# Two more blocks of V kept across the layer change, with the feed-forward weights laid around them

## The chip, the cores and the metric

One Trainium2 chip, one of its cores. The time is that of the device, in microseconds (us), from one execution of the whole program; lower is better.

## The reference

Two layers, run twice with the same weights and the same caches: attention of one new token per sequence against cached keys and values, then a gated feed-forward. Four sequences (B = 4), width 512, 32 query heads in 8 groups, 8192 cached positions, head size 128.

```python
def _A_ref(x, k_cache, v_cache, wq, wo):
    q = (x @ wq).reshape(B, Sq, Hq, Dh).transpose(0, 2, 1, 3)
    k = jnp.repeat(k_cache, rep, axis=1)
    v = jnp.repeat(v_cache, rep, axis=1)
    scores = jnp.einsum("bhqd,bhkd->bhqk", q, k) * (Dh ** -0.5)
    p = _softmax(scores, axis=-1)
    o = jnp.einsum("bhqk,bhkd->bhqd", p, v)
    return o.transpose(0, 2, 1, 3).reshape(B, Sq, Hq * Dh) @ wo
def _B_ref(x, w_gate, w_up, w_down):
    return (_silu(x @ w_gate) * (x @ w_up)) @ w_down
x = x + _A_ref(_layernorm(x), A_k_cache, A_v_cache, A_wq, A_wo)
x = x + _B_ref(_layernorm(x), B_w_gate, B_w_up, B_w_down)
# and both lines once more
```

K and V are 67.1 MB each in bf16 and each layer needs all of both; the weights are small beside them (w_gate, w_up and w_down are 512 x 1792 or its reverse).

## The kernel before, in words

**Units.** A unit u (0 to 15) is one sequence and two of the 8 key groups. K(u) and V(u) are 4096 KB each: 128 partitions by 8 blocks of 4 KB, so one block of a transfer is 512 KB. Layer 0 takes the units in the order 0 to 15, layer 1 in the order 15, 14, 13, 12, 0, 1 ... 11 (`order`).

**Room.** `kvf` holds four slots (0 to 3) of 8 blocks for K and V, a fifth slot (`QS`) that holds wq first and serves as a fifth slot in layer 1, and `wres` for part of the up weights. The program tracks each block of each slot under a name (`s1.6` is block 6 of slot 1).

**The queue.** All transfers are written out in one list, `cmds`, made by `placed`: item, slot, first and last block. SyncE issues them in that order. `pump` goes on with the list whenever `freed` gives blocks back, and an issue waits on the chip for the last readers of its room, so one that waits holds up all behind it.

**A unit's work.** VectorE (DVE) turns keys in place (`turn`, two blocks at a time as a rule), TensorE (PE) makes the scores block by block (`scores`), DVE takes the maximum (`max_p`, `max_t`), ScalarE (ACT) the exponential (`exps`), DVE turns that into `pT` (`turn_p`), and PE multiplies it with V in four parts (`values`). For the last unit of a layer the turned exponential lies in `late_pT`, at the end of the slot of the weights, instead of `pT`. `keys` and `values` put blocks of PE's work into a list that `drain` empties some microseconds late (`LAG`, and `AHEAD` for the second unit of layer 1), so that DVE runs ahead; the steps behind a unit's scores lie in `line` and are dealt out between blocks by `advance`. Each engine works in the order in which it was given instructions.

**The layer change.** What layer 0 used last is kept for layer 1 (`keep`): K(15) in slot 0, V(14) in slot 2, V(15) in slot 3; and of K(13) blocks 6 and 7 are held in the matmul memory and turned back later (`hold`, `half_kept`). Slot 1, whose last tenant is V(13), takes the feed-forward weights as soon as V(13) is used: gate (7168 elements of a partition), the rest of up, then w_down in three pieces (`WDS`; the last, `W+`, when the last unit is done with `late_pT`). The feed-forward (`ffn`) makes gate, then up, each as 14 column blocks of 4 matmuls, then the down product in 56 matmuls; it gives slot 1 back piece by piece, for K(14). `qproj` then frees the two halves of `QS` for K(13), K(15)'s scores free slot 0 for K(12), K(14)'s free slot 1 for V(13). Layer 1 ends with its own weights in slot 3.

Below, K(14) and the like always mean the loads for layer 1 unless layer 0 is named.

Of the kernel before, what the change touches and what calls it, by code (L numbers as in the profile page):

```python
# [9 lines left out]
FP32 = mybir.dt.float32  # L10
# [93 lines left out]
def bass_interleave_layers__gqa_block_cached__swiglu_ffn__decode_kernel(  # L104
# [18 lines left out]
    P = 128  # L123
# [21 lines left out]
    with ExitStack() as es:  # L145
# [14 lines left out]
        WDS = (((0, 8, 4), (8, 12, 4), (12, 14, 2)), ((0, 8, 2), (8, 12, 2), (12, 14, 2)))  # L160
        NW = len(WDS[0])

# [3 lines left out]
        assert O_WD + FO * D <= SL  # L166
        wres = kvf[:, (NSLOT + 1) * SL:]
# [19 lines left out]
        def wd_at(s, fo, k):  # L187
            return columns(s * SL + O_WD + fo * D + pick2(k).start)

        pT_w = TB * NH * QB  # L190
        assert all((w[-1][1] - w[-1][0]) * D >= pT_w for w in WDS)

        def late_pT(s):
            return kvf[:, (s + 1) * SL - pT_w:(s + 1) * SL]
# [20 lines left out]
        pT = sb("pT", [P, TB, NH, QB], BF16)  # L215

# [138 lines left out]
        cmds += [(("W", 0), W_SLOT[0], 0, NB), (("W+", 0), W_SLOT[0], NB, NB + 1)]  # L355
# [9 lines left out]
        cmds += [(("W", 1), W_SLOT[1], 0, NB), (("W+", 1), W_SLOT[1], NB, NB + 1)]  # L365

# [4 lines left out]
        def load_weight(name, i=0, s=0):  # L371
            if name == "wq":
                n = 2 * HqDh
                T.dma("sp", kv[:, QS, i * n:(i + 1) * n],
                      A_wq[i * 2 * P:(i + 1) * 2 * P, :].rearrange("(p e) f -> p (e f)", e=2), sem_w["wq"][i],
                      writes=[f"wq{i}"])
            elif name == "wo":
                src = A_wo[i * H2 * Dh:(i + 1) * H2 * Dh, :]
                T.dma("sp", wo_sb[:, i * H2:(i + 1) * H2, :].rearrange("p (c j) n -> p c (j n)", j=NA),
                      src.rearrange("(c p j) n -> p c (j n)", p=P, j=NA), sem_w["wo"][i], writes=[f"wo{i}"])  # L380
            else:
                w0 = kvf[:, s * SL:(s + 1) * SL]
                if name == "W+":
                    load_wd(w0, i, NW - 1, ["late"])
                    return
                T._wait("pool", T._need((), [f"s{s}.{NB - 1}"]))
                T.op("pool", lambda e: e.memset(late_pT(s).bitcast(FP32), 0.0), writes=["late"])
                T.dma("sp", w0[:, 0:KT * F].rearrange("p (c x) -> p c x", c=2),
                      B_w_gate.rearrange("(c p e) f -> p c (e f)", c=2, e=2), sem_w["wg"][0],
                      writes=[f"s{s}.{q}" for q in range(NB)] + ["wg"])  # L390
# [6 lines left out]
                for j in range(NW - 1):  # L397
                    load_wd(w0, i, j)

        def load_wd(w0, L, j, also=()):  # L400
            a, b, e_ = WDS[L][j]
            T.dma("sp", w0[:, O_WD + a * D:O_WD + b * D].rearrange("p (m x) -> p m x", x=e_ * D),
                  B_w_down[a * P:b * P, :].rearrange("(m p e) n -> p m (e n)", p=P, e=e_), sem_w["wd"][j],
                  writes=[f"wd{j}"] + list(also))

        def pump(most=len(cmds)):
            while issued[0] < most:
# [3 lines left out]
                else:  # L411
                    need = {(s, q) for q in range(a, b)}
# [3 lines left out]
                    if it[0] in ("W", "W+"):  # L416
                        load_weight(it[0], it[1], s)
                    else:
                        slot_of[it] = s
                        load(it, a, b, sem_s[s] if b - a == NB else part_sem())  # L420
# [4 lines left out]
        def load(it, a, b, sm):  # L425
            kind, L, u = it
            s = slot_of[it]
            gp, bt = pair_gb(u)
# [4 lines left out]
            T.dma("sp", kv[:, s, a * BW:b * BW], src[:, a * BW:b * BW], sm,  # L433
                  writes=[f"s{s}.{q}" for q in range(a, b)] + over)
# [24 lines left out]
        def finished(it, a, b):  # L459
# [24 lines left out]
        def turn(L, u, q, n):  # L484
            s = slot_of[K(L, u)]
            w = kv[:, s, q * BW:(q + n) * BW].bitcast(FP32)
            names = [f"s{s}.{i}" for i in range(q, q + n)]
# [17 lines left out]
        def scores(L, u, q):  # L505

            s = slot_of[K(L, u)]
            bk = SBK[turn_of[u]]
            w = kv[:, s, q * BW:(q + 1) * BW].rearrange("p (t c i e) -> p t c i e", t=TB, c=2, e=2)
            for c in range(4):  # L510
# [3 lines left out]
                     reads=[f"s{s}.{q}", "zq"], writes=[f"pb{bk}"], sig=(c == 3))  # L514
# [51 lines left out]
        def pT_of(L, u):  # L566
            if u == order[L][-1]:
                return late_pT(W_SLOT[L]).rearrange("p (t n x) -> p t n x", n=NH, x=QB), "late"
# [29 lines left out]
        def keys(L, u, before, lag):  # L598
# [14 lines left out]
            for q in range(NB):  # L613
                if (L, u, q) not in turned:
                    two = 0 < order[L].index(u) < NP - 1 and q % 2 == 0 and (L, u, q + 1) not in turned
# [11 lines left out]
        def values(L, u):  # L627
# [22 lines left out]
            def part(i):  # L650
# [18 lines left out]
                if i == 3:  # L669
                    more = later.pop(0)() if later else []  # L670
                    if p_name == "late":
                        freed(W_SLOT[L], NB, NB + 1)
                    done.add((L, u))
# [191 lines left out]
        def ffn(L):  # L865
# [6 lines left out]
            rooms = {"wg": room(s, 0, O_WU), "wu": room(s, O_WU, O_WD)}  # L872
            for j, (a, b, _) in enumerate(WDS[L]):
                rooms[f"wd{j}"] = room(s, O_WD + a * D, O_WD + b * D)
            names = {"wg": ["wg"], "wu": ["wu0", "wu1", "wu2"]}
            for at, wname, bk in ((wg_at, "wg", gb), (wu_at, "wu", ub)):
                for fo in range(FO):
                    if bk == gb and fo == FO // 2:
                        deviation(zero_sb, "zero")
                    f = base(L, fo)  # L880
                    for kt in range(KT):
# [3 lines left out]
                                                      start=(kt == 0), stop=(kt == KT - 1)),  # L885
                             reads=rooms[wname] + names[wname] + ["xn"], writes=[f"pb{bk}"],
                             sig=(fo == FO - 1 and kt == KT - 1))
                freed(s, *((0, 3) if wname == "wg" else (3, 4)))
# [20 lines left out]
            for j, (a, b, _) in enumerate(WDS[0]):  # L909
                k = OBK[0] if j else SBK[1]  # L910
                for nt in range(KT):
                    for fo in range(a, b):
# [3 lines left out]
                                                      start=(j < 2 and nt == 0 and fo == a),  # L916
                                                      stop=(j in (0, NW - 1) and nt == KT - 1 and fo == b - 1)),
# [86 lines left out]
```

## Time and profile before

| | before |
|---|---|
| time, median of 3 runs | 647.07 us (646.84 to 647.4) |
| profiled execution | 647.03 us, span 645.1 us from the first to the last instruction |
| mean granted clock of TensorE | 0.827 |
| transfers on the list in the layer change, W to V(13) | 19 |

The page of the profile gives the busy time of each engine, the span in 40 slices, the DMA queues, the chain of work that ended last, the costliest groups of instructions and the DMA issues. Times in the timeline and the chain are in us from the span's start. "L488" is line 488 of the kernel before: L488 turns keys, L512 is the scores' matmul, L518 the maximum, L644 the product with V, L841 qproj, L882 gate and up, L913 the down product of layer 0, L903 that of layer 1, L453 the turning back of held keys, L93 the helper that issues every transfer. A row of DMA issues ends with the time from issue to landing; a transfer has landed when the last of the 16 DMA engines is done with its part.

### The profile page before, as it was taken

The page shows a single profiled execution, that of the slowest core. Times are in us where ns is not written, and L with a number is a line of the kernel's source. Part 1 is how long each engine was busy: PE and PEld are TensorE (multiplying, and loading weights), DVE is VectorE, ACT ScalarE, POOL GpSimd, SP SyncE. Part 2 cuts the span into 40 slices and gives each one's busy share as a digit, 9 for nine tenths or more (in the row PEclk, how much of TensorE's full clock was granted, in tenths as well). Part 3 has the DMA queues.
Part 4 walks back from the last instruction along what each step waited for, and adds up shares of the span by engine and source line. Part 5 has one row for each costly group of instructions (what it writes and reads, how often), then busy time and mean ns, then how long its engine had stood idle before and what let it go on. Part 6 is the DMA issues. An engine that isn't in the chain of part 4 may idle for free.

```text
span 645.1 us, 7412 instructions
## 1 busy us (share of the span) xinstructions
PE 419.5 (65%) x3126; PEld 182.6 (28%) x3128; DVE 422.0 (65%) x591; ACT 41.2 (6%) x117; POOL 11.1 (2%) x43
## 2 busy tenths in 40 slices
PE   0683475456765746767867877777555676557877
PEld 0431122122222312222226433233122222222325
DVE  5275467456776656776962778878655677665964
ACT  0000000000000000000010010000000000000110
POOL 0000000000000000000000000000000000000000
PEclk9995887688876889767975899997778887679787
DMA  9999999999999999999999999999999999999997
GB/s 368 442 425 418 440 434 425 426 433 438 425 425 440 433 424 432 435 431 424 433 412 404 424 446 424 425 438 432 425 428 443 424 427 439 432 427 426 441 410 276
DMA packets 14704, 273.36 MB, mean 424 GB/s; under 512 B 1480, under 2 KB 1488, under 8 KB 5328
## 3 DMA queue, kind: packets, MB, share of 16 engines
q1 hardware_dynamic: 14672, 272.91, 99.1%
q8 instruction: 24, 0.39, 0.2%
q14 instruction: 8, 0.07, 0.0%
HBM read 272.90 MB, written 0.00 MB: 423 GB/s over the span
## 4 chain that ended last, share of the span: by engine, by line
DMA 62%; DVE 20%; PE 12%; issue 3%; another core or an unknown queue 1%; SPq 0%; ACTq 0%; ACT 0%; DVEq 0%
DMA kvf<-in_A_k_cache_dram 50%; DVE kvf L488 16%; DMA kvf<-in_A_v_cache_dram 11%; PE ps L512 7%; PE ps L644 2%; DMA kvf<-in_B_w_down_dram 2%; DVE pb L694 2%; PE ps L841 1%; PE ps L882 0%; DVE pb L690 0%; DVE kvf L453 0%; DVE scr L704 0%; SPq L93 0%; PE ps L523 0%
## 5 line engine op out<-in xcount | busy, mean ns | idle before, releaser
L512 PE MATMUL ps<-kvf,zq 128*128 128x512 bf16 x1024 | 297.0, 437 | 182.0 <-DVE kvf L488 178.2
L488 DVE STREAM_TRANSPOSE kvf<-kvf 128x2048 f32<-128x2048 f32 (+1 forms) x131 | 280.0, 2162 | 127.8 <-DMA kvf<-in_A_k_cache_dram 127.6
L512 PEld LDWEIGHTS ps<-kvf,zq 128*128 128x128 bf16 x1024 | 100.7, 109 | 339.7 <-DVE kvf L488 218.7
L644 PE MATMUL ps<-kvf,pT 128*32 128x512 bf16 x960 | 65.8, 396 | 1.3 <-DVE pT L576 1.3
L559 ACT ACTIVATE pb<-ps,tiny 128x512 bf16<-128x512 f32 x32 | 22.0, 688 | 529.7 <-DVE tiny L557 510.0
L576 DVE STREAM_TRANSPOSE pT<-pb 64x512 bf16<-64x512 bf16 x60 | 41.2, 687 | 3.6 <-ACT pb L559 2.6
L694 DVE SCALAR_TENSOR_TENSOR pb<-ps,tiny,pb 128x128 f32<-128x128 f32 x104 | 36.5, 351 | 4.5 <-PE ps L644 0.8
L518 DVE TENSOR_REDUCE tiny<-ps 128x1 f32<-128x512 f32 x32 | 22.0, 687 | 21.3 <-PE ps L512 21.3
L644 PEld LDWEIGHTS ps<-kvf,pT 128*32 128x32 bf16 x960 | 20.8, 98 | 31.0 <-issue 15.3
L699 PEld LDWEIGHTS ps<-sel,pb 128*128 128x128 f32 x64 | 17.3, 278 | 16.6 <-DVE pb L694 8.0
L502 POOL TENSOR_TENSOR zq<-scr,tiny 128x64 bf16<-128x64 bf16 x30 | 9.0, 299 | 563.3 <-PE ps L512 563.3
L526 DVE TENSOR_REDUCE mrm<-ps 1x8 f32<-1x128 f32 x32 | 8.8, 275 | 13.8 <-PE ps L523 13.8
L549 PEld LDWEIGHTS ps<-mrm,tiny 128*128 128x128 f32 x60 | 13.7, 234 | 9.6 <-issue 3.3
L699 PE MATMUL ps<-sel,pb 128*128 128x8 f32 x64 | 12.5, 269 | 5.5 <-DVE pb L694 5.5
L841 PE MATMUL ps<-xn,kvf 128*128 128x4 bf16 x256 | 7.4, 166 | 11.3 <-DMA kvf<-in_A_wq_dram 11.0
L549 PE MATMUL ps<-mrm,tiny 128*128 128x16 f32 x60 | 10.4, 251 | 3.1 <-ACT mrm L561 3.1
L690 DVE TENSOR_SCALAR pb<-ps,tiny 128x128 f32<-128x128 f32 x32 | 10.1, 316 | 2.6 <-PE ps L644 2.6
L760 PE MATMUL ps<-wo_sb,scr 128*4 128x512 bf16 x48 | 11.0, 379 | 0.4 <-DVE scr L729 0.4
L841 PEld LDWEIGHTS ps<-xn,kvf 128*128 128x128 bf16 x256 | 7.3, 105 | 11.6 <-DMA kvf<-in_A_wq_dram 11.2
L523 PE MATMUL ps<-identf,tiny 128*1 128x128 f32 x32 | 8.6, 270 | 1.9 <-DVE tiny L518 1.9
L561 ACT ACTIVATE mrm<-head,tiny 128x8 f32<-128x8 f32 x32 | 9.6, 300 | 1.0
L882 PE MATMUL ps<-xn,kvf 128*128 128x4 bf16 x224 | 7.3, 169 | 1.6 <-DMA kvf<-in_B_w_up_dram 1.2
(83 smaller groups left out, 113.1 us busy)
## 6 DMA issues: line engine op xcount, KB each, us to landing
kvf<-in_A_k_cache_dram SPq DMA_DIRECT2D x27, 4096.0 KB, 31.0
kvf<-in_A_v_cache_dram SPq DMA_DIRECT2D x27, 4096.0 KB, 35.3
kvf<-in_A_v_cache_dram SPq DMA_DIRECT2D x4, 2048.0 KB, 18.4
kvf<-in_A_k_cache_dram SPq DMA_DIRECT2D x7, 1024.0 KB, 9.9
kvf<-in_A_k_cache_dram SPq DMA_DIRECT2D x3, 2048.0 KB, 11.0
kvf<-in_A_wq_dram SPq DMA_DIRECT2D x2, 2048.0 KB, 18.1
wo_sb<-in_A_wo_dram SPq DMA_DIRECT2D x4, 1024.0 KB, 41.3
kvf<-in_B_w_gate_dram SPq DMA_DIRECT2D x2, 1792.0 KB, 23.7
```

The lines of the kernel that those rows point to most:

```text
L488: T.op("dve", lambda e: e.transpose(w, w), reads=names, writes=names)
L512: T.op("pe", lambda e: e.matmul(bank(bk)[:, 0:SW], lhsT=zq[:, z0:z0 + P], rhs=w[:, :, c // 2, :, c % 2], start=(q == 0 and c == 0), stop=( ...
L518: T.op("dve", lambda e: e.tensor_reduce(mx[:], bank(bk)[:, 0:SW], AX.X, ALU.max), reads=[f"pb{bk}"], writes=["mx"])
L549: T.op("pe", lambda e: e.matmul(at, lhsT=ones, rhs=mrm[:, i * H2:(i + 2) * H2], start=True, stop=True), reads=[f"m8{i}", "rsm", "onesf"], ...
L559: T.op("act", lambda e: e.activation(pb[:], bank(bk)[:, 0:SW], ACTF.Exp, bias=nm, accum_out=rs), reads=[f"pb{bk}", "nm"], writes=PB + ["rs"])
L576: T.op("dve", lambda e: e.transpose(dst, pb[hp]), reads=["pb", "row"], writes=[name])
L644: T.op("pe", lambda e: e.matmul(bank(k)[j * QB:(j + 1) * QB, q0 * Dh:q1 * Dh], lhsT=p_t[:, t, h, :], rhs=v[:, q0:q1, t, :], start=((last o ...
L690: T.op("dve", lambda e: e.tensor_scalar(into, o, own[:, q:q + 1], None, op0=ALU.mult), reads=[f"pb{k}", "own"], writes=["row"] if last els ...
L694: T.op("dve", lambda e: e.scalar_tensor_tensor(into, o, own[:, q:q + 1], into, op0=ALU.mult, op1=ALU.add), reads=[f"pb{k}", "own", iname], ...
L699: T.op("pe", lambda e: e.matmul(at, lhsT=into, rhs=sel[:], start=True, stop=True), reads=[iname, "sel"], writes=[name])
L760: T.op("pe", lambda e: e.matmul(bank(OUTB)[0:B, 0:D], lhsT=oT[:, h, :], rhs=wo_sb[:, h, :], start=(gp == groups[L][0] and r == 0), stop=(g ...
L841: T.op("pe", lambda e: e.matmul(at[:, h * B:(h + 1) * B], lhsT=wq_sb[:, kt, h * Dh:(h + 1) * Dh], rhs=xn[:, kt * B:(kt + 1) * B], start=(k ...
```

## The change

- **V(13).** Blocks 6 and 7 of V(13), which layer 0 left in slot 1, stay there (`parked`, `PARK` = 6). Layer 1 loads only blocks 0 to 5.
- **Weights of layer 0.** They now have 6 blocks of slot 1. w_down goes in five pieces: column blocks 8 to 11 and 12, 13 behind the up weights; 6 and 7 into `pT` (`Wp`, after V(14)'s product); 0 to 3 and 4, 5 (`W2`) over the first half of the gate weights, issued when that half has been used. The down product takes the pieces in this order, and GpSimd zeroes `pT` afterwards.
- **Keys of K(14).** Blocks 0 to 5 go to slot 1 in another order (2, then 3, then 4 and 5, then 0 and 1), blocks 6 and 7 to blocks 0 and 1 of slot 0 (`aside`, `home`, `lies`). They are turned singly, behind the scores of K(14)'s blocks 3 and 4 in the list of blocks. K(12)'s blocks 0 and 1, whose room that is, are loaded after V(13).
- **Gate and up.** Each is made in two halves of the contraction: the first half for all 14 column blocks, then the second half for all of them, each with names of its own to wait for. This holds for both layers.

```diff
-        WDS = (((0, 8, 4), (8, 12, 4), (12, 14, 2)), ((0, 8, 2), (8, 12, 2), (12, 14, 2)))
+        WDS = (((8, 12, 4), (12, 14, 2), (6, 8, 2), (0, 4, 4), (4, 6, 2)), ((0, 8, 2), (8, 12, 2), (12, 14, 2)))
...
+        PARK = NB - 2
+        ENDS = (PARK * BW, SL)
+        LATE = (1, 2)
+        FO_P, FO_S = WDS[0][2][:2]
+        QN = -(-FO_P * D // BW)
...
+        def wd_from(L, fo):
+            return O_WD + fo * D if L else fo * D if fo < FO_P else O_WD + (fo - FO_S) * D
...
-        cmds += [(("W", 0), W_SLOT[0], 0, NB), (("W+", 0), W_SLOT[0], NB, NB + 1)]
+        parked = {V(0, NP - 3): V(1, NP - 3)}
+        cmds += [(("W", 0), W_SLOT[0], 0, PARK), (("W+", 0), W_SLOT[0], NB, NB + 1),
+                 (("Wp", 0), W_SLOT[0], NB + 1, NB + 2)]
...
-        cmds += [(K(1, us[1]), s, a, b) for a, b in ((0, 3), (3, 4), (4, 6), (6, NB))]
+        cmds += [(("W2", 0), s, NB + 2, NB + 3)]
+        cmds += [(K(1, us[1]), s, a, b) for a, b in ((QN, 3), (3, 4), (4, PARK), (0, QN))]
         cmds += [(K(1, us[2]), QS, 0, NB // 2), (K(1, us[2]), QS, NB // 2, NB - 2)]
+        cmds += [(K(1, us[1]), 0, PARK, NB)]
         seq = loads(1, 3)
         ring = (0, 1, 3, QS, 2)
-        cmds += placed(seq, ring, {0: twos, 1: half, len(seq) - 1: ends})
+        n = NB - PARK
+        rest = placed(seq, ring, {0: lambda it, s: [(it, s, 0, n), (it, s, n, 4), (it, s, 4, 6), (it, s, 6, NB)],
+                                  1: lambda it, s: [(it, s, 0, QH), (it, s, QH, PARK)],
+                                  len(seq) - 1: ends})
+        cmds += rest[1:6] + rest[:1] + rest[6:]
...
+        aside = K(1, us[1])
+        def home(it, a, b):
+            if it == aside and a >= PARK:
+                return 0, a - PARK, b - PARK
+            return slot_of[it], a, b
...
+                if name == "W2":
+                    for j in range(3, len(WDS[i])):
+                        load_wd(w0, i, j, ["wg0"] if j == 3 else [])
+                    return
...
+            elif it in parked and b > PARK:
+                slot_of[parked[it]] = slot_of[it]
+                freed(slot_of[it], a, PARK)
             else:
-                freed(slot_of[it], a, b)
+                freed(*home(it, a, b))
...
-                if (L, u, q) not in turned:
+                if (L, u, q) not in turned and not (K(L, u) == aside and q >= PARK):
...
                 blocks.append((0.9, lambda q=q: block(q)))
+                if K(L, u) == aside and 3 <= q < 3 + NB - PARK:
+                    blocks.append((0.0, lambda q=q - 3 + PARK: turn(L, u, q, 1)))
...
-            for at, wname, bk in ((wg_at, "wg", gb), (wu_at, "wu", ub)):
+            for at, wname, bk, ks in ((wg_at, "wg0", gb, (0, KT // 2)), (wg_at, "wg1", gb, (KT // 2, KT)),
+                                      (wu_at, "wu0", ub, (0, KT // 2)), (wu_at, "wu1", ub, (KT // 2, KT))):
...
+                if wname == "wg0":
+                    deviation(zero_sb, "zero")
+                    if not L:
+                        freed(s, NB + 2, NB + 3)
+                elif wname[-1] == "1":
+                    freed(s, *((0 if L else QN, 3) if wname == "wg1" else (3, 4)))
...
             for j, (a, b, _) in enumerate(WDS[0]):
-                k = OBK[0] if j else SBK[1]
+                k = OBK[0] if j > 2 else SBK[1]
...
-                if not j:
-                    freed(s, 4, 6)
+                if j == 1:
+                    freed(s, 4, PARK)
+                if j == 2:
                     add_to_x(bank(k)[:, 0:XB], f"pb{k}")
-            freed(s, 6, NB)
+                    T.op("pool", lambda e: e.memset(pTf.bitcast(FP32), 0.0), writes=["pT"])
+            freed(s, 0, QN)
             add_to_x(bank(k)[:, 0:XB], f"pb{k}")
```

`hold`, `qproj`, `keys` otherwise, `values` otherwise and layer 0 up to V(13) are as they were.

More of the change, by code (lines that the diff above doesn't have):

```diff
@@ L187, in wd_at, with late_pT @@
         def wd_at(s, fo, k):
-            return columns(s * SL + O_WD + fo * D + pick2(k).start)
+            o = pick2(k).start
+            if FO_P <= fo < FO_S:
+                o += (fo - FO_P) * D
+                return pTf[:, o:o + 2 * (P - 1) + 1:2]
+            return columns(s * SL + wd_from(0, fo) + o)
+        def wd_from(L, fo):
+            return O_WD + fo * D if L else fo * D if fo < FO_P else O_WD + (fo - FO_S) * D
         pT_w = TB * NH * QB
-        assert all((w[-1][1] - w[-1][0]) * D >= pT_w for w in WDS)
-        def late_pT(s):
-            return kvf[:, (s + 1) * SL - pT_w:(s + 1) * SL]
+        assert all((w[l][1] - w[l][0]) * D >= pT_w for w, l in zip(WDS, LATE))
+        def late_pT(L):
+            end = W_SLOT[L] * SL + ENDS[L]
+            return kvf[:, end - pT_w:end]
         def room(s, a, b):
@@ L411, in pump @@
                 else:
-                    need = {(s, q) for q in range(a, b)}
+                    if it[0] in "KV" and (it, a) != (aside, PARK):
+                        slot_of[it] = s
+                    at = home(it, a, b) if it[0] in "KV" else (s, a, b)
+                    need = {(at[0], q) for q in range(at[1], at[2])}
                     if not need <= free:
@@ L427, in load @@
             s = slot_of[it]
+            at, names = lies(it, a, b)
             gp, bt = pair_gb(u)
@@ L432, in load @@
             q_gone.update(over)
-            T.dma("sp", kv[:, s, a * BW:b * BW], src[:, a * BW:b * BW], sm,
-                  writes=[f"s{s}.{q}" for q in range(a, b)] + over)
+            T.dma("sp", at, src[:, a * BW:b * BW], sm, writes=names + over)
         def freed(s, a, b):
```

68 lines of the change are left out of this document (40 added, 28 removed).

## The prediction

> **What bounds the kernel now.** I read the page first, for the engines' shares and the DMA rows.
>
> ```profile
> PE 419.5 (65%) x3126; PEld 182.6 (28%) x3128; DVE 422.0 (65%) x591; ACT 41.2 (6%) x117; POOL 11.1 (2%) x43
> DMA  9999999999999999999999999999999999999997
> q1 hardware_dynamic: 14672, 272.91, 99.1%
> q8 instruction: 24, 0.39, 0.2%
> HBM read 272.90 MB, written 0.00 MB: 423 GB/s over the span
> ```
>
> No compute engine is busy for more than 65% of the span, while the 16 DMA engines are busy in every one of the 40 slices, the layer change in the middle included, and only the last slice sinks. The kernel is a stream of 272.9 MB. What a change is worth is then (a) the bytes that it takes from the stream, (b) what each transfer costs beyond its bytes, and (c) whether the queue ever runs empty, because SyncE issues in order and stops at a transfer whose room isn't free.
>
> For the price of bytes I took the chain of waits where the stream is undisturbed, and the DMA issues in the same stretch.
>
> ```profile
> 472.14 43.32 DMA kvf<-in_A_k_cache_dram
> 530.42 43.31 DMA kvf<-in_A_k_cache_dram
> kvf<-in_A_k_cache_dram SPq DMA_DIRECT2D x4, 4096.0 KB, 43.3
> kvf<-in_A_v_cache_dram SPq DMA_DIRECT2D x3, 4096.0 KB, 35.8
> ```
>
> The first number is the issue, the second the time until it landed. The two K transfers land at 515.46 and 573.73. Seven transfers were issued from the one through the other, so their landings are six transfers apart: 58.27 / 6 = 9.71 us for 4096 KB, or 2.43 us for 1024 KB.
>
> Then I read the chain at the layer change, where the change acts.
>
> ```profile
> 338.15 12.51 DMA kvf<-in_B_w_down_dram
> 350.70 0.39 PE ps L913 x8
> 357.98 2.29 DVE kvf L453 x2
> 360.27 8.77 DVE kvf L488 x4
> 419.61 37.58 DMA kvf<-in_A_k_cache_dram
> ```
>
> The last piece of the down weights lands at 350.66, the feed-forward ends on it, and from there to 419 the chain runs through compute. That does not make compute the bound there: the page's DMA row has a 9 in all these slices. It says only where compute would have to be quicker to feed the queue earlier, and the queue does not need that as long as it holds work. How much it holds is read from SyncE's issues in the timeline:
>
> ```profile
> 345.22 0.33 SPq L93 DMA_DIRECT2D kvf<-in_A_k_cache_dram  x1
> 348.30 0.33 SPq L93 DMA_DIRECT2D kvf<-in_A_k_cache_dram  x1
> 349.88 0.33 SPq L93 DMA_DIRECT2D kvf<-in_A_k_cache_dram  x1
> 351.11 0.33 SPq L93 DMA_DIRECT2D kvf<-in_A_k_cache_dram  x1
> 354.51 0.33 SPq L93 DMA_DIRECT2D kvf<-in_A_k_cache_dram  x1
> 361.31 0.33 SPq L93 DMA_DIRECT2D kvf<-in_A_k_cache_dram  x1
> 372.18 0.33 SPq L93 DMA_DIRECT2D kvf<-in_A_v_cache_dram  x1
> 377.84 0.33 SPq L93 DMA_DIRECT2D kvf<-in_A_k_cache_dram  x1
> ```
>
> and from the DMA issues of 345 to 378, with their time to landing:
>
> ```profile
> kvf<-in_A_k_cache_dram SPq DMA_DIRECT2D x7, 1024.0 KB, 9.9
> kvf<-in_A_v_cache_dram SPq DMA_DIRECT2D x2, 2048.0 KB, 11.3
> kvf<-in_A_k_cache_dram SPq DMA_DIRECT2D x1, 4096.0 KB, 19.5
> kvf<-in_A_k_cache_dram SPq DMA_DIRECT2D x1, 2048.0 KB, 11.0
> kvf<-in_A_k_cache_dram SPq DMA_DIRECT2D x1, 1536.0 KB, 9.1
> kvf<-in_A_k_cache_dram SPq DMA_DIRECT2D x1, 512.0 KB, 7.3
> ```
>
> **Term 1, the bytes: -2.43 us.** Blocks 6 and 7 of V(13) stay in slot 1 over the layer change, so the second layer loads 6 of its 8 blocks: 2 x 512 KB = 1024 KB less. No other byte disappears: the weights are the same bytes in other pieces, and K(14) and K(12) are loaded whole.
>
> **Term 2, more transfers: +0.13 us.** From the landing at 350.66 to the one at 377.84 + 19.5 = 397.34 lie 46.68 us and 13 transfers (the six rows above), 19,456 KB. At 9.71 us per 4096 KB that is 46.12 us, so a transfer costs 0.56 / 13 = 0.043 us beyond its bytes. The change makes 18 transfers where there were 15 before K(0): down weights 5 for 3, K(14) 5 for 4, the others as many. 3 x 0.043 = 0.13.
>
> Here a page of the Trainium skill speaks against the change. "DMA: Bandwidth & Descriptors" asks for at least 1 MiB per transfer (section Rules for kernel authors) and fits about 2.0 us plus the bytes for each (section Anatomy of one DMA, for transfers that GpSimd issues); by it the three more would be an estimated +6.0 us, and the sum +3.6 instead of -2.30. This trace disagrees as long as transfers stand behind one another: 0.043 us each.
>
> **Term 3, an empty queue: 0.** The late transfers are moved to where less is queued, so I follow the queue on the new order, always by the engine that lands last. The feed-forward of layer 0:
>
> ```profile
> 342.78 1.07 PE L882 MATMUL ps<-xn,kvf 128*128 128x4 bf16 x28 [0.36 <-DVE pb L818]
> 346.33 1.95 PE L882 MATMUL ps<-xn,kvf 128*128 128x4 bf16 x56 [1.18 <-DMA kvf<-in_B_w_up_dram]
> 348.85 0.99 PE L913 MATMUL ps<-pb,kvf 128*128 128x4 bf16 x32 [0.58 <-DVE pb L896]
> 350.06 1.01 PE L913 MATMUL ps<-pb,kvf 128*128 128x4 bf16 x24 [0.22 <-DMA kvf<-in_B_w_down_dram]
> ```
>
> 768 KB of the down weights ("W2") now wait until the first half of the gate weights is used, that is for 28 matmuls, which end at 343.85 now as then (28 of 56 either way; the two matmuls of the deviation come behind them in both). What is queued ahead of W2 is what was queued before less these 768 KB, so it lands at 350.66 - 1.82 = 348.84. W2 is issued 5.0 us ahead of its turn and lands at 350.7 as the last weights did before. So the feed-forward still ends near 351. Making up by halves lets 28 of its 56 matmuls run in the 1.18 us that the trace shows as a wait; that moves K(14)'s fourth block about 1 us forward from 348.30 at most, and nothing waits for it.
>
> Behind W2, with the issue times of before as the late bound, each transfer's turn comes as follows: K(14) block 2 issued 345.2, turn 350.7; block 3 issued 348.3, turn 352.0; blocks 4 and 5 issued 349.9, turn 353.2; blocks 0 and 1 issued 351.1 (after the last down matmul), turn 355.7; K(13) issued 354.5, turn 358.2; K(14) blocks 6 and 7 issued 361.3 into the room that K(15) leaves in slot 0, turn 365.6; three pieces of K(12); V(13) issued 372.2, turn 375.5; its second piece and K(12)'s first, then K(0) issued 377.8, turn 385.3. The thinnest places have 3.3 us. What a transfer needs from nothing is bounded by the output's:
>
> ```profile
> 643.57 0.29 SPq L974 DMA_DIRECT2D out_dram<-pb  x1
> SPq L975 <- DMA out_dram<-pb: 1.0, 1, 1.0
> ```
>
> 0.29 + 1.0 = 1.3 us from issue to landed with nothing ahead. 3.3 is more than 1.3, so the term is 0. It can't go below 0, since the stream has no hole to fill. Its other bound is 1.5 us, by a view that shows the 16 engines not quite level:
>
> ```profile
> 352.00:354.00 2.00, 1.65 (x55) 1.56 (x55) 0.61 (x4) 0.00 (x0) 0.00 (x0) 0.50 0.92 346
> ```
>
> The last two columns are DMA share and GB/s: 0.92 and 346 where the queue was thin already. Some engines ran dry for a moment. The landings show no loss, since a transfer lands with its slowest engine, which had work. With 1024 KB less in the queue from 348 to 378 this will be seen more; were it to reach the slowest engine at two or three of the thin places for half a microsecond, it would cost 1.0 to 1.5. I take 0, as the nearest row (the landings) shows none.
>
> **Edits at no cost, and their cover.** DVE's turns of K(14):
>
> ```profile
> L488 DVE STREAM_TRANSPOSE kvf<-kvf 128x2048 f32<-128x2048 f32 x115 | 261.4, 2294 | 127.7 <-DMA kvf<-in_A_k_cache_dram 127.6
> L488 DVE STREAM_TRANSPOSE kvf<-kvf 128x1024 f32<-128x1024 f32 x16 | 18.7, 1211 | 0.1
> L387 POOL MEMSET kvf<- 128x512 f32 x2 | 1.1, 529 | 32.6 <-DVE kvf L488 20.3 <-PE ps L644 12.2
> ```
>
> Four pairs become three and two singles: 2 x 1.21 - 2.29 = +0.13 us of DVE, and the maximum of K(15) comes one pair (2.2) earlier. Blocks 6 and 7 land near 368 and are turned near 370, behind K(15)'s exponential; if they came later, the scores of K(14) would wait, and K(0)'s load with them, which has 7.5 us in hand (377.8 against 385.3). Closer is blocks 0 and 1: landed at 358.2, first turned at 360.27, 2.1 us. Of GpSimd's work there is one more zeroing, of pT, at 0.53; its next user is K(15)'s turned exponential some 20 us on.
>
> **The end** of layer 1 keeps its length: the same 112 matmuls in another order and the same transfers. Its chain:
>
> ```profile
> 588.64 42.40 DMA kvf<-in_A_v_cache_dram
> 641.21 1.73 PE ps L903 x32
> ```
>
> It hangs from V's landing at 631.04, and all behind that moves with it.
>
> **Sum.** -2.43 + 0.13 + 0 = -2.30 us. The profiled execution took 647.03 (span 645.1), the median is 647.07, so 0.04 apart; 644.7 against the profile, 644.8 against the median. A difference of 0.2%, 1.3 us, is what a measurement of this kernel can tell from none.
>
> **Rivals.** (A) The queue gets too thin: at K(13), at V(13) or at both the slowest engine idles for 1.0 to 2.3 us together, and a third to all of the gain goes: 645.8 to 647.1. For it: the 0.92 above, with 1024 KB more queued than there will be. Against it: 3.3 us in hand. (B) Slower: the layer change runs dry outright. If the feed-forward ended over 2.0 us later (3.3 - 1.3), say because W2's pieces land late, qproj and each transfer behind it would be issued to idle engines; six transfers from W2 to K(13), each alone at 1.3, lose 7.8, less 2.3: 652.6. From 4.3 us of slip on it is slower than before. Against it: W2 is issued 5.0 us ahead of its turn. The page's fixed cost would come true here, and its own sum (above) would be 650.7. (C) The bytes don't go (V(13) is loaded whole after all): HBM read stays 272.9 MB, 647.2. The diff speaks against it. (D) Luck of the instruction packets: the q8 row gives 0.2% of 16 x 645.1 us for 24 packets, 0.86 us each, and every one holds up one engine. One more or one fewer on the slowest engine is 0.9 us either way; the instructions hardly change, so this goes into the range.
>
> **How the numbers follow.** Forecast 0.75 (644.8, own range 643.8 to 645.7 by D); A 0.13; B 0.07; C 0.02; D piled on part of A 0.03. Faster by over 0.2% (under 645.8): the forecast and a little of A, 0.78. Same: most of A, C, D, 0.13. Slower: B and the worst of A with D, 0.09. The range takes D's lower end and half of A: 643.7 to 646.4.
>
> **What would show it.** Right: HBM read of 271.85 MB, 9s through the middle slices, W2 issued at 344, its landing and the last down matmul at 351, K(0) landing 2.3 us earlier (395.0), and every later landing too. Wrong: in the middle slices an 8 or less, W2 issued after 346, K(13)'s first half landing after 363.5, or a DVE wait for K(14)'s blocks 0 and 1 beyond 360.3. A time over 646.4 with 271.85 MB read would mean that bytes aren't the price.

## The result, and the profile after

The changed kernel takes 646.18 us (median of 15 runs, 645.13 to 647.56) against 647.07 (15 runs, 646.84 to 647.95): a ratio of 0.9984, with a 95% interval of 0.9977 to 0.9992. It is faster, but by 0.9 us where 2.3 were forecast, which is below the 1.3 us that the prediction called distinguishable. Its profiled execution took 646.18 with a span of 644.3 us; before it was 647.03 and 645.1.

The page of the changed kernel, DMA rows as before:

```profile
DMA  8999999999999999999999999999999999999996
q1 hardware_dynamic: 14976, 271.86, 99.0%
q8 instruction: 24, 0.39, 0.2%
HBM read 271.85 MB, written 0.00 MB: 422 GB/s over the span
```

The bytes went as forecast (272.90 to 271.85 MB). Every middle slice still has its 9: at this grain nothing seems lost. But the mean rate is 422 GB/s where it was 423, on fewer bytes.

The chain of waits at the layer change:

```profile
344.10 6.46 DMA kvf<-in_B_w_down_dram
350.61 0.39 PE ps L974 x8
360.18 6.59 DVE kvf L539 x3
370.55 1.16 DVE kvf L539
373.06 1.26 DVE kvf L539
419.31 35.32 DMA kvf<-in_A_k_cache_dram
```

(L539 turns keys, L974 is the down product.) The late weights land at 350.56, the feed-forward ends on them at the same time as before, the three pairs of K(14) start at 360.18, and the two single turns stand at 370.5 and 373.1, behind the exponential. Every step is where the prediction put it. The landing of K(0) is not; SyncE's issue of it and its time to landing:

```profile
377.66 0.33 SPq L93 DMA_DIRECT2D kvf<-in_A_k_cache_dram  x1
kvf<-in_A_k_cache_dram SPq DMA_DIRECT2D x1, 4096.0 KB, 18.4
```

It lands at 396.1, against 397.3 before and 395.0 in the forecast. Almost half of the gain is missing already here. Where it went shows in the view by stretches, for the 14 us from 346 to 360; the last three columns are the granted clock, the DMA share and GB/s. Before:

```profile
346.00:360.00 14.00, 11.19 (x266) 9.15 (x267) 4.87 (x15) 0.56 (x2) 0.00 (x0) 0.50 1.03 414
```

After:

```profile
346.00:360.00 14.00, 10.60 (x238) 8.34 (x239) 4.74 (x15) 0.56 (x2) 0.53 (x1) 0.50 1.01 385
```

29 GB/s less over 14 us is 0.41 MB that did not come. At 432 GB/s (4096 KB in the 9.71 us of the prediction) that is 0.94 us. The DMA share beside it hardly moves (1.03 to 1.01), since packets are recorded longer here: the 26 packets of 8 KB that began from 350 to 352, the first of K(14)'s blocks 4 and 5, took 0.55 us in the mean, where the median of that size is 0.31. That these times hold the wait of idle engines is likely, not shown.

The end, from the chain: the last V but one piece, and the last matmuls.

```profile
586.09 43.48 DMA kvf<-in_A_v_cache_dram
640.50 1.60 PE ps L964 x56
```

V lands at 629.57, 1.47 earlier than before (631.04). So the profiled execution's -0.85 is the -1.47 up to V and a loss of 0.6 behind it.

### The profile page after: what moved, and what is told of

The parts are those of the page before. It is cut to its first block, busy times and chain, and to the rows that moved or that the text cites. A ratio compares the mean times of both kernels' runs of the same rounds, so it can differ in the third digit from the quotient of the medians.

```text
span 644.3 us, 7421 instructions
## 1 busy us (share of the span) xinstructions
PE 413.2 (64%) x3126; PEld 178.3 (28%) x3128; DVE 421.2 (65%) x592; ACT 41.2 (6%) x117; POOL 11.6 (2%) x44
## 3 DMA queue, kind: packets, MB, share of 16 engines
HBM read 271.85 MB, written 0.00 MB: 422 GB/s over the span
## 4 chain that ended last, share of the span: by engine, by line
DMA 61%; DVE 22%; PE 10%; issue 4%; another core or an unknown queue 1%; SPq 0%; DVEq 0%
DMA kvf<-in_A_k_cache_dram 49%; DVE kvf L539 17%; DMA kvf<-in_A_v_cache_dram 11%; PE ps L563 5%; PE ps L698 2%; DVE pb L750 2%; DMA kvf<-in_B_w_down_dram 1%; PE ps L938 1%; DVE pb L746 1%; PE ps L897 1%; SPq L93 0%; DVE pT L627 0%; DVE scr L760 0%; PE ps L841 0%
## 5 line engine op out<-in xcount | busy, mean ns | idle before, releaser
L563 PE MATMUL ps<-kvf,zq 128*128 128x512 bf16 x1024 | 289.7, 428 | 186.9 <-DVE kvf L539 182.2
L539 DVE STREAM_TRANSPOSE kvf<-kvf 128x2048 f32<-128x2048 f32 (+1 forms) x132 | 280.3, 2147 | 127.1 <-DMA kvf<-in_A_k_cache_dram 126.9
L563 PEld LDWEIGHTS ps<-kvf,zq 128*128 128x128 bf16 x1024 | 98.1, 107 | 344.0 <-DVE kvf L539 228.3
L755 PEld LDWEIGHTS ps<-sel,pb 128*128 128x128 f32 x64 | 15.8, 256 | 14.9 <-DVE pb L750 7.2
L897 PE MATMUL ps<-xn,kvf 128*128 128x4 bf16 x256 | 7.4, 166 | 11.3 <-DMA kvf<-in_A_wq_dram 10.9
L600 PEld LDWEIGHTS ps<-mrm,tiny 128*128 128x128 f32 x60 | 12.0, 205 | 8.3 <-DVE scr L760 3.2
L698 PE MATMUL ps<-kvf 128*32 128x512 bf16 (+2 forms) x96 | 5.5, 358 | 4.3 <-DMA kvf<-in_A_v_cache_dram 4.1
```

The lines of the kernel that those rows point to most:

```text
L539: T.op("dve", lambda e: e.transpose(w, w), reads=names, writes=names)
L563: T.op("pe", lambda e: e.matmul(bank(bk)[:, 0:SW], lhsT=zq[:, z0:z0 + P], rhs=w[:, :, c // 2, :, c % 2], start=(q == 0 and c == 0), stop=( ...
L600: T.op("pe", lambda e: e.matmul(at, lhsT=ones, rhs=mrm[:, i * H2:(i + 2) * H2], start=True, stop=True), reads=[f"m8{i}", "rsm", "onesf"], ...
L698: T.op("pe", lambda e: e.matmul(bank(k)[j * QB:(j + 1) * QB, q0 * Dh:q1 * Dh], lhsT=p_t[:, t, h, :], rhs=v[:, q0:q1, t, :], start=((last o ...
L755: T.op("pe", lambda e: e.matmul(at, lhsT=into, rhs=sel[:], start=True, stop=True), reads=[iname, "sel"], writes=[name])
L897: T.op("pe", lambda e: e.matmul(at[:, h * B:(h + 1) * B], lhsT=wq_sb[:, kt, h * Dh:(h + 1) * Dh], rhs=xn[:, kt * B:(kt + 1) * B], start=(k ...
```

## The experiments

Theory L: the bytes are worth their 2.43 us, and the loss comes from DMA engines that ran dry in the thinner queue. Rival B: 1024 KB are worth only about 1 us here. Others are named with their runs. The changed kernel's reference points are 646.18 and, beside the last run, 645.94.

**Bytes without the thin queue.** The kernel before, with the last block pair of V(13) left out of the second layer's load (that part of the product is then made from other data, the keys that lie in those blocks):

```diff
-        cmds += placed(seq, ring, {0: twos, 1: half, len(seq) - 1: ends})
+        cmds += placed(seq, ring, {0: twos, 1: lambda it, s: [(it, s, 0, 4), (it, s, 4, 6)], len(seq) - 1: ends})
```

> The kernel before, but layer 1 loads only blocks 0 to 5 of V(13); blocks 6 and 7 of that slot are left with the keys that lie there, so this part of the product is made from other data. The queue before V(13) is exactly that of the kernel before; only 1024 KB are missing. Theory L (the bytes are worth 2.43 us, and the change lost over half of that because the thinner queue at the layer change let the DMA engines that are ahead run dry, so that they lost their lead and a later delay of any one of them shows): K(0) lands at 395.0, 2.4 earlier than before (397.4), and so does the last V (628.6 for 631.0); time 644.6 to 645.3, the spread from the clock at the end. Rival B (1024 KB less are worth only about 1 us, whatever the queue, because something else bounds the stream): time 646.0 to 646.3, last V near 630.

Measured 644.40 (5 runs, 644.4 to 644.72), ratio 0.996 (0.9947 to 0.9972). Its stretch, and its K(0):

```profile
346.00:360.00 14.00, 11.17 (x266) 9.15 (x267) 4.47 (x15) 0.56 (x2) 0.00 (x0) 0.50 1.04 413
```

```profile
377.87 0.33 SPq L93 DMA_DIRECT2D kvf<-in_A_k_cache_dram  x1
kvf<-in_A_k_cache_dram SPq DMA_DIRECT2D x1, 4096.0 KB, 17.2
```

413 GB/s as before, K(0) at 395.1 as the forecast had it, and 2.66 us gained. Rival B falls: the bytes are worth their full price when the queue is left as it was.

**The thin queue without the saved bytes.** The changed kernel, with V(13) written whole:

```diff
-                                  1: lambda it, s: [(it, s, 0, QH), (it, s, QH, PARK)],
+                                  1: half,
...
-                freed(slot_of[it], a, PARK)
+                freed(slot_of[it], a, b)
```

> The changed kernel with V(13) loaded whole: blocks 6 and 7 are kept over the layer change and then written once more with the same data. All of the new order and its thin queue, none of the saved bytes. Theory L: 2.43 later than the changed kernel, 648.6 (648.2 to 649.0); so slower than the kernel before by 1.0 to 1.9. Rival B (bytes worth about 1 us): 647.0 to 647.3, as the kernel before.

Measured 648.21 (11 runs), ratio 1.002 (1.0011 to 1.0028): slower than before by 1.1. It reads as many bytes as the kernel before.

```profile
346.00:360.00 14.00, 10.58 (x241) 8.27 (x239) 5.02 (x15) 0.56 (x2) 0.53 (x1) 0.50 1.01 386
```

386 GB/s, the changed kernel's 385. Together the two give -2.66 + 1.15 = -1.5, where the changed kernel has -0.9 to -1.1: most of the missing gain is in the thin queue. The 0.4 to 0.6 that is left lies within the intervals (that of the changed kernel reaches down to -1.5), so it points at nothing else.

**The thin queue alone.** Of the changed kernel's edits none, only the order of K(14)'s pieces in the kernel before:

```diff
-        cmds += [(K(1, us[1]), s, a, b) for a, b in ((0, 3), (3, 4), (4, 6), (6, NB))]
+        cmds += [(K(1, us[1]), s, a, b) for a, b in ((2, 3), (3, 4), (4, 6), (6, NB), (0, 2))]
```

> The kernel before, with K(14)'s blocks 0 to 2 no longer loaded in one piece when gate is done: block 2 is issued then, blocks 0 and 1 last, after the last down matmul. The same bytes and the same work, one transfer more; only the queue is thinner by 1024 KB from 345 to 351. Theory L: the engines that are ahead run dry between 350 and 358 and lose 1 to 1.5 us of their lead, so that later delays show: K(0) lands at 397.8 to 398.5 (397.4 before), time 647.5 to 648.2, and the DMA share of 350 to 358 falls below the 1.0 of before. Rival S (the loss comes from transfers issued late at V(13) and K(12), or from the smaller pieces, 0.04 each): 647.1.

Measured 648.83 (6 runs, 648.47 to 649.51), ratio 1.0032 (1.002 to 1.0044): 1.8 us slower from holding 1024 KB back for six microseconds.

```profile
346.00:360.00 14.00, 11.44 (x266) 9.15 (x267) 5.35 (x16) 0.58 (x3) 0.00 (x0) 0.50 0.97 376
```

376 against 414 GB/s is 0.53 MB or 1.2 us. The direction is theory L's and not that of rival S, but the size was expected at 0.5 to 1.1 and is 1.8; the profiled execution, the fastest of its runs, lost 1.4 (648.47 for 647.03). Why the median run lost more than that isn't settled. The edit has a side effect: the turns wait for blocks 0 and 1, and V(13) is issued at 373.46 instead of 372.18. It isn't what cost the time: by the completion marks (explained below) the mean of the 16 engines was 1.15 us behind the kernel before at K(13)'s last piece already, and 1.24 at V(13)'s.

**Half the size.** One block of V(13) kept instead of two:

```diff
-        WDS = (((8, 12, 4), (12, 14, 2), (6, 8, 2), (0, 4, 4), (4, 6, 2)), ...
+        WDS = (((4, 12, 4), (12, 14, 2), (2, 4, 2), (0, 2, 2)), ...
...
-        PARK = NB - 2
+        PARK = NB - 1
```

> The changed kernel with one block of V(13) kept instead of two (512 KB less to load, 512 KB more room for the weights: down weights in four pieces, of which one of 256 KB late). Theory L: bytes worth 1.21 us; the queue is thinned by half as much, and the engines lose less of their lead, so the loss of 0.8 us at the landing of K(0) shrinks to 0.1 to 0.5: K(0) lands at 396.2 to 396.7, time 645.9 to 646.6 with the end as it falls. If the loss is a step that comes with any thinning: 646.7 to 647.0. If the loss were in proportion to the bytes (rival B): 646.6.

Measured 646.32 (11 runs), ratio 0.9987 (0.9978 to 0.9996). By its time this lies where theory L put it, but not clear of the 646.6 of rival B. K(0) landed at 397.6, later than the 396.2 to 396.7 expected, in a profiled execution that was the slowest of the 11 (647.09). In the stretch that is thinned the loss is about halved:

```profile
346.00:360.00 14.00, 9.75 (x236) 7.99 (x237) 3.93 (x15) 0.56 (x2) 0.53 (x1) 0.50 1.02 401
```

401 GB/s is 13 less than before, where the changed kernel has 29 less. By the marks, counted at equal bytes, the mean of the engines was 0.45 us late at K(13)'s last piece (1.04 in the changed kernel). Another 0.4 came at K(12)'s first piece, which was issued at 364.79, 1.3 us before the first engine had finished what was ahead of it (3.7 in the changed kernel). So this run has a second thin place, and its whole loss doesn't measure the first.

**The order by halves.** Alone in the kernel before (both layers), and undone in layer 1 of the changed kernel:

```diff
-            for at, wname, bk in ((wg_at, "wg", gb), (wu_at, "wu", ub)):
+            for at, wname, bk, ks in ((wg_at, "wg0", gb, (0, KT // 2)), (wg_at, "wg1", gb, (KT // 2, KT)),
+                                      (wu_at, "wu0", ub, (0, KT // 2)), (wu_at, "wu1", ub, (KT // 2, KT))):
...
```

> The kernel before with gate and up made by halves in both layers and nothing else. Forecast and theory L: the halves move K(14)'s fourth block about 1 us forward and nothing waits for it, so no change: 646.9 to 647.3. If the halves lengthened the end of layer 1: 647.5 to 647.8.

Measured 647.08 (10 runs) against 646.99, ratio 1.0001 (0.9992 to 1.001): nothing, as forecast.

```diff
...
+            if L:
+                passes = ((wg_at, "wg1", gb, (0, KT)), (wu_at, "wu1", ub, (0, KT)))
...
```

> The changed kernel, with layer 1's gate and up made as before (each column block's four matmuls together). From the last V's landing to the end the profile shows 12.5 us of chain where the kernel before has 11.9. If that is TensorE's clock (0.5 from 632 on where it was 1.0 until 636): no difference to the changed kernel, 645.8 to 646.5, and matmul times at the end go with the granted clock. If it is the order by halves: 0.5 to 0.6 faster than the changed kernel, 645.5 to 645.7.

Measured 645.73 (9 runs, 645.14 to 646.04), ratio 0.9979 (0.997 to 0.9989), just under the range for the clock and just over that for the order. The profiles decide. The stretch from 632 to 634, second last but one column the granted clock; first the kernel before, then the changed one, then this one:

```profile
632.00:634.00 2.00, 1.36 (x21) 0.64 (x20) 1.38 (x4) 0.00 (x0) 0.00 (x0) 1.00 1.02 415
```

```profile
632.00:634.00 2.00, 1.54 (x24) 1.16 (x26) 0.44 (x3) 0.00 (x0) 0.00 (x0) 0.50 1.01 405
```

```profile
632.00:634.00 2.00, 1.66 (x52) 1.37 (x52) 0.37 (x2) 0.00 (x0) 0.00 (x0) 1.00 1.00 397
```

In the changed kernel's profiled execution TensorE was at half clock there, in the others at full. Its chain from V's landing to the end took 13.1 us (629.57 to 642.70; the 12.5 of the expectation counts to the last matmul); this kernel's took 12.5 (629.20 to 641.74), and so did that of the kernel with one block kept, which has the halves and the full clock (631.20 to 643.69). So the halves cost nothing that the time shows, and the 0.6 us at the end of that execution go with the clock.

**The place of the late turns.** The changed kernel, with K(14)'s blocks 6 and 7 turned as a pair ahead of the maximum:

```diff
-                if (L, u, q) not in turned and not (K(L, u) == aside and q >= PARK):
+                if (L, u, q) not in turned:
...
-                if K(L, u) == aside and 3 <= q < 3 + NB - PARK:
-                    blocks.append((0.0, lambda q=q - 3 + PARK: turn(L, u, q, 1)))
```

> The changed kernel, with K(14)'s blocks 6 and 7 turned as a pair ahead of the maximum of K(15), as before. They land at 368.4 and DVE would be ready at 366.8, so DVE waits about 1.7 us, and the scores of K(14), V(13)'s loads and K(0)'s come 1.5 to 2 us later. V(13) had 4 us in hand, K(0) over 7. By the forecast this is hidden: as the changed kernel, 645.7 to 646.5. Theory L: V(13)'s issue moves near its turn and takes 0 to 0.5 more of the lead: 646.2 to 646.8.

Measured 649.20 (10 runs; two of them near 646.6), ratio 1.0026 (1.0015 to 1.0036): 3 us slower than the changed kernel, where almost nothing was expected. DVE's turn of the pair, with its wait in brackets, SyncE's issue of V(13), and the stretch of 375 to 385:

```profile
368.91 2.31 DVE L539 STREAM_TRANSPOSE kvf<-kvf 128x2048 f32<-128x2048 f32 x1 [2.15 <-DMA kvf<-in_A_k_cache_dram]
```

```profile
376.35 0.33 SPq L93 DMA_DIRECT2D kvf<-in_A_v_cache_dram  x1
```

```profile
375.00:385.00 10.00, 8.26 (x54) 2.93 (x53) 4.99 (x7) 0.83 (x3) 0.30 (x1) 0.83 0.78 305
```

In the changed kernel V(13) was issued at 371.39 and that stretch reads:

```profile
375.00:385.00 10.00, 6.66 (x56) 2.75 (x55) 8.96 (x12) 0.00 (x0) 0.30 (x1) 1.00 1.04 439
```

The wait of 2.15 and the pair's 2.31 stand ahead of the maximum, and PE, which works in order, holds K(14)'s third block behind the maximum's transpose. V(13)'s issue moved by 5.0, not by 1.5 to 2. PE's transpose and the four matmuls behind it, here and then in the changed kernel:

```profile
371.85 0.37 PE L574 MATMUL ps<-identf,tiny 128*1 128x128 f32 x1 [2.87 <-DVE tiny L569]
372.02 1.91 PE L563 MATMUL ps<-kvf,zq 128*128 128x512 bf16 x4
```

```profile
368.88 0.27 PE L574 MATMUL ps<-identf,tiny 128*1 128x128 f32 x1
368.99 1.04 PE L563 MATMUL ps<-kvf,zq 128*128 128x512 bf16 x4
```

3.0 of the 5.0 us are the wait. The other 1.9 are TensorE's clock: it was granted at 0.50 from 372 to 378, where the changed kernel had 1.00, and the matmuls took nearly twice as long. No expectation had this. Two of the ten runs took 646.4 and 646.8; whether the clock stayed up in them no trace shows.

V(13) was issued when all 16 engines were done (the last at 376.28), and the queue ran dry: 134 GB/s less over 10 us is 1.34 MB, 3.1 us. This is the kind of rival B of the prediction, a transfer issued to idle engines, at one place instead of six. The price was higher than B's 1.3 us:

```profile
kvf<-in_A_v_cache_dram SPq DMA_DIRECT2D x1, 2048.0 KB, 7.4
```

7.4 us from issue to landing, where the bytes take 4.86 (2 x 2.43).

**A place made thicker.** The changed kernel, with layer 1's qproj taking wq by quarters, K(13) loaded in three pieces:

```diff
-        cmds += [(K(1, us[2]), QS, 0, NB // 2), (K(1, us[2]), QS, NB // 2, NB - 2)]
+        cmds += [(K(1, us[2]), QS, q, q + 2) for q in (0, 2, 4)]
...
+                for h, kt in ([(h, kt) for kt in (2 * c, 2 * c + 1) for h in range(Hq)] if L else
+                              [(h, kt) for h in range(Hq) for kt in (2 * c, 2 * c + 1)]):
...
```

> The changed kernel, with qproj of layer 1 working through wq by quarters, so that K(13) is loaded in three pieces of two blocks, the first 0.9 us earlier. Theory L: one of the thin places, K(13), gets 0.9 us more in hand, and the leading engines lose 0.3 us less there; the others stay. K(0) lands 0 to 0.4 earlier than in the changed kernel (396.0), time 645.7 to 646.3. If K(13) was the place that cost it all: 645.3 or less.

Measured 645.67 (11 runs), ratio 0.9981 (0.9973 to 0.999); K(13) was not the place that cost it all. At K(0) the quarters brought nothing of the 0 to 0.4 that was expected: the mean of the engines was 394.90, in the changed kernel 394.85.

```profile
346.00:360.00 14.00, 10.53 (x238) 8.34 (x239) 4.59 (x15) 0.56 (x2) 0.53 (x1) 0.50 1.01 388
```

**The changed kernel once more, and a version with both.** The last one is the quarters and six filling matmuls for three while PE waits for the last V (`fill(3)` to `fill(6)`).

> The changed kernel as it is, beside the next one. Theory L: the 16 DMA engines' mean landing of K(0) is again 1.0 to 1.3 us later than the saved bytes would give (394.7 to 394.9 for 393.65), and the time 645.7 to 646.6 with the end as it falls.

> The changed kernel with qproj by quarters and with six instead of three of the matmuls that only keep TensorE busy while it waits for the last V. If TensorE's clock at the end is what made the last 12.5 to 13.1 us vary, the clock stays at 1.0 beyond 634 and the stretch from the last V's landing to the end is 12.0 to 12.5 in this run: time 645.2 to 645.8. If the clock does not follow from this work, or the three matmuls delay the product with V: 645.7 to 646.5.

Measured 645.94 (11 runs, 645.17 to 646.38), ratio 0.9982 (0.9973 to 0.9991), and 645.40 (9 runs, 645.01 to 645.59), ratio 0.9972 (0.9962 to 0.9982). The second is the fastest version here that computes everything, and beats the kernel before; that it beats the changed kernel isn't shown, since the intervals overlap. Its reason did not hold: the six matmuls delayed the product with V, which had landed at 628.7, by 0.4 us, and the stretch to the end was 13.0 us, not 12.0 to 12.5.

```profile
627.66 1.46 PE L678 MATMUL ps<-wo_sb 128*128 128x512 bf16 x6
629.05 0.83 PE L698 MATMUL ps<-kvf 128*32 128x384 bf16 x16
```

It isn't the delay that made it 13.0, though. Here, as in the run of the changed kernel beside it, the end hung on the last weights; the chain of that one:

```profile
606.15 34.56 DMA kvf<-in_B_w_down_dram
640.76 0.60 PE ps L964 x12
```

The weights landed at 641.35 there and at 640.62 here, and the output was issued 1.1 us later in both, as in the kernel before (642.44 and 643.57). In the changed kernel's first profiled execution, at half clock, it was 1.7 us later.

**The 16 engines one by one.** Each transfer leaves 16 completion marks in the trace, one for each DMA engine. For each kernel's profiled execution, when the first, the mean and the last of them came, in us, for the last piece of layer 0's V(15), K(0) and the last weights of layer 1:

```
kernel              V(15)                  K(0)                   last weights
before              333.9  335.20  337.4   394.6  396.08  397.4   638.1  640.46  642.4
changed             333.9  335.19  337.3   393.8  394.85  396.0   637.9  639.26  641.0
changed, again      333.9  335.24  337.3   394.1  394.88  396.6   637.7  639.30  641.4
bytes only          333.9  335.22  337.1   392.2  393.64  395.1   635.7  638.12  640.0
halves only         333.9  335.21  337.4   394.7  396.09  397.3   638.2  640.48  642.4
thin only           334.0  335.23  337.2   396.3  397.23  398.1   639.8  641.63  643.1
thin, in before     333.9  335.30  337.1   396.8  397.30  398.8   640.4  641.76  643.8
one block kept      333.9  335.20  337.1   395.1  395.95  397.6   638.7  640.39  642.6
pairs               333.9  335.26  337.3   397.8  398.10  398.4   641.4  642.66  644.9
old order, layer 1  334.0  335.24  337.2   393.7  394.66  395.7   637.3  639.10  640.7
quarters            333.9  335.21  337.2   394.1  394.90  396.6   638.0  639.33  641.4
quarters and fill   333.9  335.25  337.3   394.1  394.64  395.1   637.7  639.18  640.6
```

Up to the layer change all are alike: the first engine is 3.2 to 3.5 us ahead of the last. In the two kernels with the full queue the mean at K(0) is what the bytes give (393.64 is 2.44 less than 396.08). With the thinned queue it is later by 1.21 (changed, against bytes only), 1.15 (thin only, against before), 1.22 (thin in before) and, for 2.43 / 2 less bytes, 1.08 (one block); by 1.0 to 1.3 in the last three rows and the changed kernel's second run. The same 1.0 to 1.3 stand at the end (pairs apart). The first engine lost most (1.6 us, changed against bytes only), the last one 0.9.

The marks also tell where. From the piece ahead of W2 to K(13)'s first piece, the time between marks beyond 2.43 us for 1024 KB adds up to 2.5 us for the first engine, 1.9 in the mean and 0.9 for the last in the changed kernel; with the bytes alone, from the last down weights to K(13)'s first piece, to 1.0, 0.8 and 0.3. In the changed kernel each of these transfers was issued 1.5 to 2.8 us before the first engine had finished the one ahead, and 3.7 to 5.8 before the last had; with the bytes alone 2.2 to 3.9 and 5.8 to 7.0. What a transfer needs from nothing shows at V(13) in the run with the pairs: issued to idle engines, it was done 1.9 us (first engine) to 2.6 us (last) later than its bytes alone take. The first engine often had no more than that in hand.

## Why the prediction was right and wrong

**The bytes: right.** -2.43 was forecast, -2.66 measured with the queue untouched, K(0) within 0.1 of its forecast landing.

**More transfers: not contradicted.** The 0.13 us is too small to be seen by itself in the time. The packets' own durations (medians of 0.084 us for 2 KB, 0.31 for 8 KB, 0.61 for 16 KB), summed over all packets, give 0.13 us more per engine for the thin queue with all its bytes than for the kernel before: smaller pieces aren't what cost 1.2. The +6.0 us for three more transfers, worked out from the Trainium skill's "DMA: Bandwidth & Descriptors" (section Anatomy of one DMA), did not come: the kernel with three more and no fewer bytes lost 1.1.

**The empty queue: wrong, and the step is the sentence "a transfer lands with its slowest engine, which had work", with the 0 that was taken from it.** The issue times that it worked with held within 1.5 us, the turns within 1.1, and the last engine did have work by them, 3.7 us at the thinnest place, K(13). What it missed is that each of the 16 engines works through its own share, and that those ahead reach the end of a thin queue first: the first engine had 1.5 to 2.8 us in hand. The second error is the price of a start. 1.3 us was read from the output's 4 KB; 2048 KB issued to idle engines took 1.9 to 2.6 beyond their bytes. Added up, 3.5 us of lead and 1.9 for a start, the last engine needs an estimated 5.4 us in hand for the first to go on without a stop. The kernel before had 5.4 to 7.0 there and lost 0.8 us in the mean, the changed kernel had 3.7 to 5.8 and lost 1.9. Against the kernel with the bytes alone that was 1.2 us at K(0); the prediction's own upper bound was 1.5. The prediction saw the row that says so (0.92 at 352) and read it as harmless, because the landings showed no loss in that place.

An engine's lead is not idle reserve, though. In the table the last engine trails the mean at the end by 1.8 to 2.1 us in both runs of the changed kernel, by 2.0 in the kernel before and by 1.4 to 2.2 in all. The distance comes out much alike whether the leaders waited or not, so what the mean lost at 350 is lost at the end. What sets the engines apart isn't shown. The trace suggests 24 packets of 16 KB on the queue of the instructions (the q8 row), most of them 1.0 to 1.1 us long. One begins at 370.8, and the next piece of K(12), 1024 KB, landed 3.05 us behind the one ahead of it in the changed kernel, against 2.5 in the kernel before, where such a packet came at the same place. In the mean of the engines that piece took 2.57 us in both, 0.09 more than the next one, which is 1.4 us if a single engine was held up. That the packets do this is argued from the times alone; the trace doesn't name the engine of a packet, and no run moved them.

**The cover of the turns: right, and thinner than told.** The edit cost nothing in its place. Undone, it costs 3 us: the prediction named K(0)'s load, with 7.5 us in hand, as what would wait, and passed over V(13)'s, which is released by the same scores and had 3.3 by its own list. TensorE's half clock behind the wait, 1.9 of V(13)'s 5.0 us, was in no forecast.

**Halves and the end: right in length, not in what sets it.** The halves cost nothing that the time shows. The prediction hung the end on V's landing. It hangs as much on the last 256 KB of the weights, which landed 1.1 us before the output's issue in the kernel before and in most runs. From V's landing to the end that made 12.5 us, and 13.0 to 13.1 where the last engine was later with the weights (the changed kernel's second run, the quarters, the quarters with the fill). In the first profiled run of the changed kernel the granted clock fell at about 631: the weights landed 1.4 us earlier than before, the output was issued only 0.8 earlier, and 0.6 went to the clock.

**The sum.** On the profiled execution: -2.43 + 0.13, then +0.8 from the thin queue as it stood at the last V (-1.47 measured there), then +0.6 by the clock: -0.9, measured -0.85. The forecast's time was missed by 1.4 us. The range holds the result only because half of rival A was put into it; the forecast's own part of it, 643.8 to 645.7, doesn't. Of the rivals (A) came true, by its time (645.8 to 647.1) and its kind; it was priced on the slowest engine at K(13) and V(13), and it acts on the leading ones, from W2 to K(13). It deserved far more than 0.13.

## What to carry to other kernels

Where a stream of transfers is the bound, room kept for data that saves a load is taken from the queue's depth: measure what is queued at the thinnest place against the lead of the fastest DMA engine (here 3.5 us) and the start of a transfer of the real size (here 1.9 to 2.6) together, not against the start of a 4 KB transfer. A row of slices with a 9 in each, and landings on time, don't show the loss; GB/s over the thin stretch and the mean of the engines' completion marks do. Before trusting a move of bytes, run the bytes alone and the thin queue alone: two small edits split -0.9 into -2.7 and +1.1 to +1.8.

## What the runs showed of the hardware that was not expected

- The 16 DMA engines of one queue drift apart: in the kernel before by 3.5 us at V(15) and by 4.3 at the last weights.
- Holding back 1024 KB for 6 us, with the last engine still supplied by the issue times, cost 1.8 us of 647.
- 2048 KB issued to 16 idle engines landed 7.4 us later, 2.6 beyond their bytes; the output's 4 KB landed 1.3 us after the issue began.
- GB/s fell from 414 to 385 in the thin stretch while the DMA share fell only from 1.03 to 1.01.
- In the run with the pairs TensorE stood idle for 2.9 us, and the granted clock was 0.50 from 372 to 378: four matmuls took 1.91 us instead of 1.04. That the idling lowered the clock isn't shown.
- Six 0.24 us matmuls meant to keep TensorE's clock up (1.46 us together) did not keep it up longer than three: it was at 1.0 to 634 and at 0.88 from 634 to 636, against 0.98 in the run of the changed kernel beside it, in one profiled execution of each.
